# V Wo of all heads ahead of the first queries, the last FFN halves one step sooner, the last gates on ScalarE, the last deferred store behind the last transpositions

## The chip, the cores and the metric

The kernel runs on one core of a Trainium2 chip. The time is the device time of one execution in microseconds; the median of three runs of the kernel before is 559.36 (559.25, 559.36 and 560.31). The profile is of one further execution. In what follows PE is TensorE, DVE is VectorE, ACT is ScalarE, POOL is GpSimd and SP is SyncE.

## What is computed

```python
xn  = layernorm(x)                                  # 2048 x 448
q   = xn @ wq                                       # 16 heads of 256
k,v = the last 512 rows of the caches               # 8 heads, each used by two query heads
s   = concat_h(softmax(q k^T / 16) v) @ wo          # 2048 x 448
g   = silu((gelu(xn @ w_gate) * (xn @ w_up)) @ w_down)
out = x + s * g
```

## The kernel before

The kernel has no scheduler: a small planner (`Plan`) records operations in the order in which the Python code names them, gives each engine its own in that order, and derives the semaphore waits from declared buffers. What an engine does first is therefore decided by the order of the code alone. All matmuls go through one line, L384 in `mms`, so they are told apart by their operands (bank<-kT,qT are scores, bank<-xq,wq and wqr queries, bank<-vw,pT and vw,sS the product with V Wo, bank<-wd,actT the FFN's down product, bank<-woa,vTa or wob,vTb V Wo itself). ScalarE's plain activations go through L378, plain DMAs through L372, transposing DMAs through L375.

The work has three stages.

First, the FFN: layernorm, gate and up products, gelu, and the down product of each of 16 row tiles of 128. A down product is two halves of seven matmuls 128x448 (`down_mm`), and behind the second half ACT's tanh (L378) and a DVE operation (L581) make the gate of that tile (`down_gate`), which `store_g` sends to DRAM.

Second, for each of 16 heads, V Wo is computed ahead, so that the attention product is with V Wo instead of V and Wo in turn. `vw_head` runs four pairs of matmuls into four PSUM banks; each is evacuated by ACT (L713, L719) and, for two of the four, by DVE as well (L715); DVE's three sums (L726) follow. L713 of the second pair waits until L715 of the first has read what it shares. The heads are put between the down halves of tiles 8 to 13 in the list `order`. Head 13 uses banks 2, 3, 6 and 7, heads 14 and 15 both use banks 0 to 3. Between heads 14 and 15 stand the queries of steps 0 and 1 (banks 7 and 6) and ACT's evacuation of them to qT (`q_evac`).

Third, the attention loop: 128 steps, one for each block of 256 rows and each head. Step n computes the scores S(n) of two tiles of 128 rows (`s_jobs`, PSUM banks 4, 5 and 6 in turn, so a tile takes the bank of the tile three before), the queries of step n + 2 (`q_jobs`; in the first four steps in banks 7 and 1, later in 7), and, from step 4 on, the product PV(n - 4) with V Wo (banks 0 to 3). The matmuls use 64 rows each; `halves` writes the order of the lower and the upper half of the rows, side by side. DVE then takes the row minimum of each tile (L852, the scores are negated), ACT the exponential (L857, with its sum), DVE the reciprocal (L863) and POOL the norm (L873). SP transposes the result, 256 rows at once, by DMA (L375) into pT, and three steps after its own step DVE makes four sums of it (L888, `sums`). PV multiplies pT and these sums by V Wo in seven products, as a fast matrix multiplication does, and sums over heads in PSUM.

In steps 0 to 3 there is no PV yet; behind their scores stand the four down halves of tiles 14 and 15 (banks 0 and 2), with the gates made in steps 1 and 3.

Once a block of 256 rows has had its 16 heads, its banks are evacuated (L947) and finished over the next nine steps: POOL sums (L955), DVE the gate (L964, into `tmp`), POOL the addition of x (L974, into `ofin`). Stores of the result and loads for the next tiles wait in a list `moves`, from which one is issued on SP's queue in each step.

The last block is handled apart. In step 125 POOL scales the last two gates into `tmp` (`gates_scaled`, L1034). After the loop the last step's norm is split (tile 0 by POOL, L1122, tile 1 by ACT), each with its own half transposition. The heads of the last four steps are multiplied directly, four matmuls 128x448 for each step and tile: eight for step 124, eight for step 125, then steps 126 and 127 for tile 14 and for tile 15. DVE and POOL (L1107) put the rest together, and SP stores tiles 14 and 15.

Of the kernel before, what the change touches and what calls it, by code (L numbers as in the profile page):

```python
# [5 lines left out]
ACT = mybir.ActivationFunctionType  # L6
ALU = mybir.AluOpType
# [159 lines left out]
def bass_recurrent_scan__sliding_block_cached__geglu_ffn__prompt_kernel(  # L167
# [36 lines left out]
    with es:  # L204
# [364 lines left out]
        def down_mm(t, o, wr, f0, f1):  # L569
            c, t4 = divmod(t, 4)  # L570
            mms([(o, actT[c % 2][:, f, t4 * P:(t4 + 1) * P], wd[:, f, :], f == 0, f == NF - 1)
                 for f in range(f0, f1)], [b_wd] + b_actT[c % 2], wr)
# [156 lines left out]
        def vw_head(h, banks, last=True):  # L729
            K.reuse(b_vw[h])  # L730
            for j, i in zip((0, 2, 1, 3), banks):
                vw_mm(h, j, i)
            if last:
                vw_sums(h)
# [61 lines left out]
        def halves(lo, up):  # L796


            t, todo = [0, 0], (list(lo), list(up))
            while todo[0] or todo[1]:  # L800
                u = 0 if todo[0] and (not todo[1] or t[0] <= t[1]) else 1
                i, c0, c1, l, r, st, sp, reads = todo[u].pop(0)
                t[u] += c1 - c0 + 6
                other = half_of[i][1 - u]
                half_of[i][u] = mms([(bank[i][:, c0:c1], l, r, st, sp)], reads, [b_ps[i]],
                                    [] if other is None else [other])
# [3 lines left out]
        def q_jobs(n, e):  # L810

            c, h = divmod(n, Hq)
            y, i = c % 2, bq(n)
            if e == 1 and 2 <= n < 2 + LAG:
                i = 1
            out = ([], [])
            reads = b_wql[h // HG] + [b_xq[y]]
            for u in range(2):
                rows = slice(R * u, R * u + R)
                for k in [2, 1, 0] + ([NK] if u == e else []):  # L820
                    l = wqr[rows, h, :] if k == NK else wq[rows, k, h * Dh + e * P:h * Dh + (e + 1) * P]
                    out[u].append([i, e * CW, (e + 1) * CW, l, xq[rows, y, k, :], False, False, reads])
            return out
# [100 lines left out]
        def flat(x):  # L924
            return [z for y in x for z in y]
# [69 lines left out]
        for k in order:  # L995
            if isinstance(k, float):
                t, f = int(k), 0 if k == int(k) else NF // 2
                i = 4 + t % 2
                down_mm(t, bank[i][:, 0:D], [b_ps[i]], f, f + NF // 2)
                if f:  # L1000
                    down_gate(t, bank[i][:, 0:D], [b_ps[i]])
                    store_g()
            elif k < 14:
                vw_head(k, banks4())
                if k in (8, 10):
                    y = k // 10
                    K.reuse(b_xq[y:y + 1])
                    load_xq(y)
            elif k == 14:
                vw_head(k, (0, 1, 2, 3))  # L1010
                js = [[q_jobs(n, e) for e in range(2)] for n in range(2)]
                js[0][0][1][0][5] = js[1][1][0][0][5] = True
                js[0][0][0][-1][6] = js[1][1][1][-1][6] = True
                halves(js[1][1][0] + js[1][0][0], js[0][0][1] + js[0][1][1])
                halves(js[0][1][0] + js[0][0][0], js[1][0][1] + js[1][1][1])
                K.reuse(flat(b_qT))
                for n in range(2):
                    q_evac(n)
            else:
                vw_head(k, (0, 1, 2, 3))  # L1020
        K.reuse(b_p32 + flat(b_pn) + b_pT[:3] + flat(b_sS[:2]) + b_tmpr + b_g2r)

        VW12 = {NST - Hq + 6 + i: Hq - LAG + i for i in range(LAG)}
# [5 lines left out]

        ends_at = ((NT - 2) % NXR, (NT - 1) % NXR)  # L1030

        def gates_scaled():
            for s, y in enumerate(ends_at):
                K.op("pool", lambda e, s=s, y=y: e.tensor_scalar(  # L1034
                    tmp[:, s, :], gr[:, y, :], sc[:, 1:2], 1.0, op0=ALU.mult, op1=ALU.mult),
                    (b_gr[y], b_sc), (b_tmp[s],))

        todo, stores, ready, last_sum = [], [], [], []
        for n in range(NST):
            h, m = n % Hq, n - LAG  # L1040
            c = n // Hq
            more = n + 2 < NST
            ends = m >= 0 and m % Hq == Hq - 1
            if n == LAG:
                store_g()
                K.reuse(b_pT[3:] + b_sS[2])
            s0, s1 = s_jobs(n, 0, True), s_jobs(n, 1, not more)
            for t in ready:
                store_out(t)
            ready, stores = stores, []  # L1050
            if moves:
                moves.pop(0)()
            if more:
                q0, q1 = q_jobs(n + 2, 0), q_jobs(n + 2, 1)
                q0[1][0][5] = True
                (q1[0] if m >= 0 else q1[1])[-1][6] = True
                if m < 0:
                    q1[0][0][5] = q0[0][-1][6] = True
            if m < 0:
                halves(s0[0] + q1[0] + q0[0] + s1[0], q0[1] + s1[1] + s0[1] + q1[1])  # L1060
                t, i, f = NT - 2 + n // 2, n // 2 * 2, n % 2 * NF // 2
                down_mm(t, bank[i][:, 0:D], [b_ps[i]], f, f + NF // 2)
            else:
                one, two, all_ = pv_plan(m)
                if more:
                    halves(s0[0] + one + q0[0] + q1[0] + s1[0] + two, q0[1] + q1[1] + s0[1] + s1[1] + all_)
                else:
                    halves(s0[0] + s1[0] + all_, one + s0[1] + s1[1] + two)
            if n >= 1:
                recip(n - 1)  # L1070
                norm(n - 1)
            row_min(n, 0)
            if more:
                q_evac(n + 2)
            if ends:
                evac(0, "dve")
                evac(2, "act")
            row_min(n, 1)
            expo(n, 0)
            expo(n, 1)  # L1080
            if 3 <= n < NST - 1:
                last_sum = [sums(n - 3, (0, 1, 2, 3))]
            if n in (1, 3):
                i = n // 2
                down_gate(NT - 2 + i, bank[2 * i][:, 0:D], [b_ps[2 * i]])
            if n == 2:
                store_g()
            if n in VW12:
                vw_plain(VW12[n])
            if n == NST - 3:  # L1090
                gates_scaled()
            if n == LAG:
                K.reuse(b_aS + b_tmp + b_ofin + b_xr + b_gr)
                for t in range(NXR):
                    load_fin(t)
            if ends:
                evac(1, "dve")
                evac(3, "act")
                todo.extend(finish(m // Hq, "pool"))
            elif todo:  # L1100
                todo.pop(0)[1]()
            if h == 2 and c >= 1 and c + 1 < NC:
                load_xq(c + 1)
        assert not todo and not stores and not ready and not moves

        def add(eng, o, a, b, reads, writes, f=ALU.add):
            K.op(eng, lambda e: e.tensor_tensor(o, a, b, f), reads, writes)  # L1107
# [23 lines left out]
        norm_tile(0, "pool")  # L1131
        K.op("dve", lambda e: e.tensor_copy(aS[:, 0:2, :], two(bank[0][:, 0:D])), (b_ps[0],), b_aS[0:2])
        norm_tile(1, "act")
        act(a[5], bank[2][:, HN:D], ACT.Copy, (b_ps[2],), b_aS[5:6])
        add("pool", a[1], a[0], a[1], b_aS[0:2], b_aS[1:2])
        add("dve", a[2], bank[1][:, 0:HN], a[0], [b_ps[1], b_aS[0]], b_aS[2:3])
# [1 line left out]
        add("dve", a[6], a[6], a[5], b_aS[5:7], b_aS[6:7])  # L1138
        add("dve", a[3], bank[1][:, HN:D], a[2], [b_ps[1], b_aS[2]], b_aS[3:4])
        add("dve", aS[:, 4:6, :], two(bank[2][:, 0:D]), aS[:, 3:4, :].broadcast_to([P, 2, HN]), [b_ps[2], b_aS[3]], b_aS[4:6])  # L1140
        gs = [two(tmp[:, s, :]) for s in range(2)]
        xs = [two(xr[:, q, :]) for q in ends_at]
        for i, k in ((1, 0), (6, 1)):
            add("pool", a[i], a[i], gs[0][:, k, :], [b_aS[i], b_tmp[0]], b_aS[i:i + 1], ALU.mult)
            add("pool", a[i], a[i], xs[0][:, k, :], [b_aS[i], b_xr[ends_at[0]]], b_aS[i:i + 1])
        o = aS[:, 4:6, :]
        add("dve", o, o, gs[1], b_aS[4:6] + b_tmp[1:2], b_aS[4:6], ALU.mult)
        add("dve", o, o, xs[1], b_aS[4:6] + [b_xr[ends_at[1]]], b_aS[4:6])
        PB = (7, 5)
        for n, t in [(n, t) for n in range(NST - LAG, NST - 2) for t in range(2)] + [  # L1150
# [8 lines left out]
        for t in range(2):  # L1159
            i, sl = PB[t], (slice(1, 7, 5), slice(4, 6))[t]  # L1160
            p = two(p32[:, t, 0:D])
            add("dve", p, two(bank[i][:, 0:D]), gs[t], [b_ps[i], b_tmp[t]], (b_p32[t],), ALU.mult)
            add(("pool", "dve")[t], two(ofin[:, t, :]), p, aS[:, sl, :], [b_p32[t]] + [b_aS[k] for k in ((1, 6), (4, 5))[t]],
                (b_ofin[t],))
            store_out(NT - 2 + t)
            moves.pop(0)()
# [55 lines left out]
```

## Time and profile before

| what | us |
|---|---|
| median of three runs | 559.36 |
| the profiled execution | 560.09 |
| its span, first to last instruction | 558.30 |
| granted TensorE clock | 1.000 |
| PE busy | 548.5 (98%) |
| DVE, ACT, POOL busy | 462.3, 341.3, 261.5 |
| first score matmul | starts at 158.67 |
| last matmul issued from | 549.74 to 554.47 |

Times in the profile are microseconds from the span's start. The page gives each engine's busy time, the chain of work that ended last, followed back from the end, and the costliest groups of instructions; the views of the trace give stretches of time, single instructions and who waited for whom. A matmul's row is its start and a modelled end, and matmuls overlap: two on different row halves run side by side, and the next starts before the last has ended. So what PE loses is read from the distance between starts, not from its busy share. DMA rows of SP are the issue alone; when the data has landed is told apart.

### The profile page before, as it was taken

To read this page: it belongs to the slowest core of one execution; us is meant where nothing else is said; L and a number is where in the kernel's file an instruction comes from. 1 tells how busy PE (TensorE), PEld (TensorE's weight loads), DVE (VectorE), ACT (ScalarE), POOL (GpSimd) and SP (SyncE) were. 2 spreads that over 40 slices of the span, in tenths; PEclk is the share of its full clock that TensorE was granted. 3 is DMA by queue.
4 is the path that set the end of the run, shared out by engine and by line. 5 is a ranking of instruction groups with operands and counts; after the bars stand their busy time and mean duration, and the time that the engine had idled before them with its cause. 6 is when DMAs were issued, how large, how long until landed. Compare 5 with 4: busy or idle time off the path is not lost.

```text
span 558.3 us, 18692 instructions
## 1 busy us (share of the span) xinstructions
PE 548.5 (98%) x7612; PEld 425.5 (76%) x7612; DVE 462.3 (83%) x1177; ACT 341.3 (61%) x811; POOL 261.5 (47%) x376
## 2 busy tenths in 40 slices
PE   8999999999999999999999999999999999999996
PEld 5544444445557999998899899999999998998883
DVE  6674979767767778898898889899888988988996
ACT  5432324467776766766767667676676666676662
POOL 1121590100004443765565476557537646654675
PEclk9999999999999999999999999999999999999999
DMA  9998999601106776478647756845865666584465
GB/s 268 182 239 148 226 310 145 128 1 44 37 18 109 121 114 108 83 105 126 100 87 138 123 78 114 127 98 94 140 104 88 111 127 106 90 139 95 79 101 85
DMA packets 187653, 66.07 MB, mean 118 GB/s; under 512 B 169120, under 2 KB 184624, under 8 KB 187568
## 3 DMA queue, kind: packets, MB, share of 16 engines
q1 hardware_dynamic: 184336, 56.96, 60.1%
q0 software_dynamic: 2464, 7.34, 4.5%
q8 instruction: 60, 0.98, 0.8%
q10 hardware_dynamic: 768, 0.57, 0.3%
q14 instruction: 25, 0.20, 0.2%
HBM read 19.76 MB, written 5.77 MB: 46 GB/s over the span
## 4 chain that ended last, share of the span: by engine, by line
PE 88%; DVE 7%; ACT 2%; issue 2%; DMA 1%; POOL 0%; DVEq 0%; ACTq 0%
PE bank L384 88%; DVE vw L726 1%; DVE vw L715 1%; DVE actT L559 1%; DMA pT<-pn 1%; ACT vw L713 1%; DVE mx L676 1%; DMA x<-in_A_x_dram 1%; DVE stats L431 1%; DVE xn L457 1%; ACT gl L378 0%; DVE sS L888 0%; DVE mn L852 0%; DVE g2a L581 0%; POOL rstd L443 0%
## 5 line engine op out<-in xcount | busy, mean ns | idle before, releaser
L384 PE MATMUL bank<-kT,qT 64*128 64x512 bf16 x1024 | 282.1, 376 | 0.5 <-ACT p L857 0.5
L873 POOL TENSOR_SCALAR pn<-p,rd 128x512 f16<-128x512 f32 x254 | 178.3, 714 | 177.8 <-DVE rd L863 177.8
L384 PE MATMUL bank<-xq,wq 64*128 64x256 bf16 x1536 | 220.9, 269 | 0.3 <-ACT vw L719 0.2
L384 PE MATMUL bank<-vw,sS 64*128 64x224 f16 x1984 | 217.5, 257 | 0.4 <-DVE sS L888 0.3
L384 PE MATMUL bank<-vw,pT 64*128 64x224 f16 (+1 forms) x1520 | 211.3, 259 | 2.0 <-DMA pT<-pn 1.5
L852 DVE TENSOR_REDUCE mn<-bank 128x1 f32<-128x512 f32 x256 | 173.3, 684 | 39.3 <-PE bank L384 33.5
L857 ACT ACTIVATE p<-bank,mn 128x512 f32<-128x512 f32 x256 | 174.8, 684 | 8.2 <-DVE mn L852 4.3
L384 PEld LDWEIGHTS bank<-vw,sS 64*128 64x128 f16 x1984 | 146.9, 94 | 19.2 <-PE bank L384 2.7
L384 PEld LDWEIGHTS bank<-xq,wq 64*128 64x128 bf16 x1536 | 141.5, 94 | 9.7 <-ACT vw L719 0.5
L384 PEld LDWEIGHTS bank<-vw,pT 64*128 64x128 f16 (+1 forms) x1520 | 142.2, 94 | 7.5 <-DMA pT<-pn 1.9
L378 ACT ACTIVATE qT<-bank 128x512 bf16<-128x512 f32 (+1 forms) x132 | 77.0, 584 | 115.9 <-PE bank L384 114.9
L384 PEld LDWEIGHTS bank<-kT,qT 64*128 64x128 bf16 x1024 | 86.9, 94 | 7.0 <-ACT p L857 1.2
L384 PE MATMUL bank<-xnT,wgu 64*128 64x512 bf16 (+2 forms) x768 | 84.4, 350 | 0.7 <-issue 0.4
L888 DVE TENSOR_TENSOR sS<-pT 128x256 f16<-128x256 f16 x248 | 73.4, 336 | 0.3 <-DMA pT<-pn 0.3
L384 PE MATMUL bank<-xq,wqr 64*128 64x256 bf16 x256 | 68.3, 269 | 0.0
L384 PEld LDWEIGHTS bank<-xnT,wgu 64*128 64x128 bf16 x768 | 36.7, 94 | 38.4 <-issue 1.2
L378 ACT ACTIVATE gl<-bank 128x512 bf16<-128x512 f32 x56 | 33.1, 597 | 48.6 <-PE bank L384 41.9
L857 ACT ACTIVATION_READ_ACCUMULATOR p<-bank,mn 128x1 f32 x256 | 50.7, 198 | 0.0
L559 DVE TENSOR_TENSOR actT<-bank,gl 128x512 bf16<-128x512 f32 x56 | 37.4, 686 | 15.6 <-PE bank L384 14.9
L888 DVE TENSOR_TENSOR sS<-sS,pT 128x256 f16<-128x256 f16 x124 | 46.8, 377 | 0.0
L384 PE MATMUL bank<-wd,actT 128*128 128x448 bf16 x224 | 45.4, 353 | 0.6 <-DVE actT L559 0.5
L955 POOL TENSOR_TENSOR aS<-aS 128x224 f32<-128x224 f32 (+1 forms) x35 | 29.8, 850 | 27.7 <-DVE rd L863 25.8
(82 smaller groups left out, 413.0 us busy)
## 6 DMA issues: line engine op xcount, KB each, us to landing
wq<-in_A_wq_dram POOLq DMA_DIRECT2D x8, 384.0 KB, 8.6
woa<-in_A_wo_dram POOLq DMA_DIRECT2D x6, 448.0 KB, 5.3
pT<-pn SPq DMA_TRANSPOSE x129, 3.1
xn_t<-xnT SPq DMA_DIRECT2D x16, 128.0 KB, 3.9
xq<-xn_t SPq DMA_DIRECT2D x8, 256.0 KB, 3.0
xr<-in_A_x_dram SPq DMA_DIRECT2D x16, 112.0 KB, 2.7
gr<-gate_t SPq DMA_DIRECT2D x16, 112.0 KB, 2.7
out_dram<-ofin SPq DMA_DIRECT2D x16, 112.0 KB, 2.0
```

Of the source, the lines that this page charges most:

```text
L378: K.op("act", lambda e, o=o, i=i: e.activation(o, i, func, scale=scale), reads, writes)
L384: ins = e.matmul(o, lhsT=l, rhs=r, start=st, stop=sp)
L431: K.op("dve", lambda e: e.bn_stats(stats[:, t, :], x4[:, t, :]), (b_x4[t],), (b_stats[t],))
L457: K.op("dve", lambda e: e.tensor_scalar(xn[:, s, lo:hi], x4[:, t, src:src + hi - lo], mv[:, t, 0:1], rstd[:, t:t + 1], op0=ALU.subtract, o ...
L559: K.op("dve", lambda e: e.tensor_tensor(actT[c % 2][:, f, :], bank[b + 1], gl[:, s, :], ALU.mult), (b_ps[b + 1], b_gl[s]), (b_actT[c % 2][ ...
L676: K.op("dve", lambda e: e.tensor_reduce(mx[:, i:i + 1], o, AX.XY, ALU.max, apply_absolute_value=True), (b,), (b_mx,))
L713: K.op("act", lambda e: e.activation(v[:, 0, jj, :], o[:, 0:HN], ACT.Copy, scale=sc[:, 0:1]), (b, b_sc), (b_vw[h][0],))
L852: K.op("dve", lambda e: e.tensor_reduce(mn[:, m:m + 1], bank[i], AX.X, ALU.min), (b_ps[i],), (b_mn[m],))
L857: K.op("act", lambda e: e.activation(p32[:, z, :], bank[i], ACT.Exp, bias=mn[:, m:m + 1], scale=-1.0, accum_out=rsum[:, 2 * r + t:2 * r + ...
L873: K.op(engs[t], lambda e, o=o, i=i, s=s: e.tensor_scalar(o, i, s, 1.0, op0=ALU.mult, op1=ALU.mult), (b_p32[z], b_rd[r]), (b_pn[y][t],))
L888: o = K.op("dve", lambda e, i=i, a=a, b=b, f=f: e.tensor_tensor(s[i], a, b, f), r, (b_sS[y][i],))
L955: K.op(eng, lambda e: e.tensor_tensor(sl[0], sl[1], sl[2], ALU.add), [b_aS[i] for i in a + b], [b_aS[i] for i in o], after=last_sum)
```

## The change

The program has the same matmuls. These things move:

- V Wo of head 15 is computed straight behind head 14, ahead of the queries of steps 0 and 1.
- The four down halves of tiles 14 and 15 stand one step sooner: the first ahead of step 0, the others behind steps 0, 1 and 2. The gates of tiles 14 and 15 are made in steps 0 and 2 (before: 1 and 3), and both are stored in step 2.
- In steps 0 to 3 the two lists given to `halves` begin with queries, and both score tiles end at the end of the step.
- The last two gates are scaled by ACT, in steps 120 and 123, into a place of their own (`gsl`, where V Wo of head 1 lay), instead of by POOL in step 125 into `tmp`.
- In the last two steps no move is issued. The one left, the store of tile 12, is issued behind the last half transposition.

```diff
-            elif k == 14:
-                vw_head(k, (0, 1, 2, 3))
-                js = [[q_jobs(n, e) for e in range(2)] for n in range(2)]
...
-                for n in range(2):
-                    q_evac(n)
             else:
                 vw_head(k, (0, 1, 2, 3))
+        js = [[q_jobs(n, e) for e in range(2)] for n in range(2)]
...
+        for n in range(2):
+            q_evac(n)
+
+        def fill(k):
+            t, i, f = NT - 2 + k // 2, (0, 2)[k // 2], k % 2 * NF // 2
+            down_mm(t, bank[i][:, 0:D], [b_ps[i]], f, f + NF // 2)
+            if f:
+                down_gate(t, bank[i][:, 0:D], [b_ps[i]])
...
-        def gates_scaled():
-            for s, y in enumerate(ends_at):
-                K.op("pool", lambda e, s=s, y=y: e.tensor_scalar(
-                    tmp[:, s, :], gr[:, y, :], sc[:, 1:2], 1.0, op0=ALU.mult, op1=ALU.mult),
-                    (b_gr[y], b_sc), (b_tmp[s],))
+        gsl, a, _ = place("gsl", [P, 2, D], F32, at=rv)
+        b_gsl = sbuf_bufs(a, D * 4, 2)
+        GS = {NST - 8: 0, NST - 5: 1}
+
+        def gates_scaled(t):
+            y = ends_at[t]
+            K.reuse(b_gsl[t:t + 1])
+            act(gsl[:, t, :], gr[:, y, :], ACT.Copy, (b_gr[y], b_sc), (b_gsl[t],), scale=sc[:, 1:2])
...
+        fill(0)
         for n in range(NST):
...
-            if moves:
+            if moves and n < NST - 2:
                 moves.pop(0)()
...
             if m < 0:
-                halves(s0[0] + q1[0] + q0[0] + s1[0], q0[1] + s1[1] + s0[1] + q1[1])
-                t, i, f = NT - 2 + n // 2, n // 2 * 2, n % 2 * NF // 2
-                down_mm(t, bank[i][:, 0:D], [b_ps[i]], f, f + NF // 2)
+                halves(q1[0] + s0[0] + q0[0] + s1[0], q0[1] + s1[1] + q1[1] + s0[1])
...
-            if n in (1, 3):
-                i = n // 2
-                down_gate(NT - 2 + i, bank[2 * i][:, 0:D], [b_ps[2 * i]])
+            if n < 3:
+                fill(n + 1)
             if n == 2:
                 store_g()
             if n in VW12:
                 vw_plain(VW12[n])
-            if n == NST - 3:
-                gates_scaled()
+            if n in GS:
+                gates_scaled(GS[n])
...
         norm_tile(1, "act")
+        while moves:
+            moves.pop(0)()
```

In the end's operations `gsl` replaces `tmp`; nothing else changes there.

More of the change, by code (lines that the diff above doesn't have):

```diff
@@ L1008, in bass_recurrent_scan__sliding_block_cached__geglu_ffn__prompt_kernel @@
                     load_xq(y)
-            elif k == 14:
-                vw_head(k, (0, 1, 2, 3))
-                js = [[q_jobs(n, e) for e in range(2)] for n in range(2)]
[L1012 to L1016, printed above, removed]
-                for n in range(2):
-                    q_evac(n)
             else:
                 vw_head(k, (0, 1, 2, 3))
+        js = [[q_jobs(n, e) for e in range(2)] for n in range(2)]
+        js[0][0][1][0][5] = js[1][1][0][0][5] = True
+        js[0][0][0][-1][6] = js[1][1][1][-1][6] = True
+        halves(js[1][1][0] + js[1][0][0], js[0][0][1] + js[0][1][1])
+        halves(js[0][1][0] + js[0][0][0], js[1][0][1] + js[1][1][1])
+        K.reuse(flat(b_qT))
+        for n in range(2):
[5 more added lines that the diff above has]
+                down_gate(t, bank[i][:, 0:D], [b_ps[i]])
         K.reuse(b_p32 + flat(b_pn) + b_pT[:3] + flat(b_sS[:2]) + b_tmpr + b_g2r)
@@ L1103, in bass_recurrent_scan__sliding_block_cached__geglu_ffn__prompt_kernel @@
                 load_xq(c + 1)
-        assert not todo and not stores and not ready and not moves
+        assert not todo and not stores and not ready
         def add(eng, o, a, b, reads, writes, f=ALU.add):
@@ L1140, in bass_recurrent_scan__sliding_block_cached__geglu_ffn__prompt_kernel @@
         add("dve", aS[:, 4:6, :], two(bank[2][:, 0:D]), aS[:, 3:4, :].broadcast_to([P, 2, HN]), [b_ps[2], b_aS[3]], b_aS[4:6])
-        gs = [two(tmp[:, s, :]) for s in range(2)]
+        gs = [two(gsl[:, s, :]) for s in range(2)]
         xs = [two(xr[:, q, :]) for q in ends_at]
         for i, k in ((1, 0), (6, 1)):
-            add("pool", a[i], a[i], gs[0][:, k, :], [b_aS[i], b_tmp[0]], b_aS[i:i + 1], ALU.mult)
+            add("pool", a[i], a[i], gs[0][:, k, :], [b_aS[i], b_gsl[0]], b_aS[i:i + 1], ALU.mult)
             add("pool", a[i], a[i], xs[0][:, k, :], [b_aS[i], b_xr[ends_at[0]]], b_aS[i:i + 1])
         o = aS[:, 4:6, :]
-        add("dve", o, o, gs[1], b_aS[4:6] + b_tmp[1:2], b_aS[4:6], ALU.mult)
+        add("dve", o, o, gs[1], b_aS[4:6] + b_gsl[1:2], b_aS[4:6], ALU.mult)
         add("dve", o, o, xs[1], b_aS[4:6] + [b_xr[ends_at[1]]], b_aS[4:6])
@@ L1161, in bass_recurrent_scan__sliding_block_cached__geglu_ffn__prompt_kernel @@
             p = two(p32[:, t, 0:D])
-            add("dve", p, two(bank[i][:, 0:D]), gs[t], [b_ps[i], b_tmp[t]], (b_p32[t],), ALU.mult)
+            add("dve", p, two(bank[i][:, 0:D]), gs[t], [b_ps[i], b_gsl[t]], (b_p32[t],), ALU.mult)
             add(("pool", "dve")[t], two(ofin[:, t, :]), p, aS[:, sl, :], [b_p32[t]] + [b_aS[k] for k in ((1, 6), (4, 5))[t]],
```

## The prediction

> **What bounds the kernel now.** The page comes first: TensorE (PE) is busy for nearly the whole span. A time is therefore won or lost only where PE waits.
>
> ```profile
> PE 548.5 (98%) x7612; PEld 425.5 (76%) x7612; DVE 462.3 (83%) x1177; ACT 341.3 (61%) x811; POOL 261.5 (47%) x376
> ```
>
> Second, the chain that ended last, asked for 150 to 182 us, where V Wo, the first queries and steps 0 to 4 lie (start, us, what):
>
> ```profile
> 155.16 0.41 DVE vw L726
> ...
> 155.90 0.38 DVE vw L726
> 156.28 0.37 DVE vw L715
> ...
> 157.65 0.97 ACT qT L378 x2
> ...
> 161.78 0.61 DVE mn L852
> ...
> 162.41 0.79 ACT p L857 x2
> ...
> 163.33 10.10 PE bank L384 x74
> ...
> 173.45 0.63 DVE g2r L581
> ...
> 174.13 7.87 PE bank L384 x100
> ```
>
> Until 163 the chain runs on DVE and ACT, which evacuate V Wo; PE joins late. After that PE sets the pace, apart from one wait for the gate of tile 15 (g2r). How much PE loses is read from the table of stretches (the first number after the stretch is its length):
>
> ```profile
> 158.67:160.84 2.17, 2.02 (x23) 1.18 (x23) 1.28 (x4) 2.06 (x5) 0.00 (x0) 1.00 0.00 0
> ...
> 162.27:164.72 2.45, 1.99 (x23) 1.32 (x23) 1.20 (x4) 1.73 (x5) 0.55 (x1) 1.00 0.00 0
> ...
> 166.15:167.89 1.74, 1.74 (x24) 1.36 (x23) 0.79 (x3) 1.14 (x4) 0.00 (x0) 1.00 0.68 133
> ...
> 172.48:176.38 3.90, 3.40 (x52) 2.72 (x53) 2.27 (x6) 1.76 (x5) 1.36 (x2) 1.00 0.44 97
> 176.38:179.37 2.99, 2.99 (x54) 2.75 (x49) 2.44 (x8) 2.02 (x6) 1.36 (x2) 1.00 0.70 132
> ```
>
> Steps 0, 1 and 2 do equal work; step 2, at 1.74, is undisturbed. So step 0 loses 0.43 and step 1 0.71. Step 4 takes 3.90 where step 5 takes 2.99: 0.91 lost. Together 2.05 us.
>
> Third, the same chain for the end:
>
> ```profile
> 542.17 0.62 DVE sS L888
> ...
> 542.84 1.96 PE bank L384 x25
> 544.80 4.89 DMA pT<-pn
> ...
> 549.74 4.73 PE bank L384 x24
> ```
>
> The last matmuls stand from 548.26 to 549.74 (the waits give 1.48) for the transposition of step 125, which POOL's norm let start at 544.80 and which took 4.89 us.
>
> **Head: V Wo of head 15 ahead of the queries.** No matmul is added or removed. Head 15 goes to banks 0 to 3, which head 14 also uses, so its first matmul waits for DVE's L715 of head 14. That one starts at 156.20, behind the sums of head 13, and ends at 156.65. Before, PE did the queries (155.18 to 157.05, 1.87) meanwhile. Now PE stands from 154.92 (last issue of head 14 at 154.73 plus the 0.19 between issues) to 156.72. Head 15 then needs bank 2, which L715 frees at 157.71, and ends issuing at 158.53; the queries follow to 160.40. Before, both were done and step 0 began at 158.67: PE is 1.73 behind.
>
> What it buys, with the filler counted (each down half takes 1.43, 160.84 to 162.27, whatever its place): the first half lies at 160.40 to 161.83. Its bank 0 is free at 159.23 and it hides the evacuation of qT (two of 0.54, from 160.52). Step 0 then starts at 161.83 with bank 1 long free, and its 0.43 is gone. The sums of head 15 end at 161.45, ahead of the scores, so row minimum and exp follow at once. In the trace of before, bank 4 came free 1.64 after the first row minimum began (161.69 to 163.33). With scores ready at 163.75 this gives 165.42, and step 1 asks for that bank 0.32 into a start at 165.00: 0.10 lost, where 0.71 was.
>
> The new order puts the queries first and both score tiles last, so less lies between scores and the next step's bank. The gate of tile 14 (tanh 0.54, then DVE 0.62, from 165.86) now stands ahead of step 1's row minimum: bank 6 is free at 168.77, wanted at 168.59, 0.18 lost in step 2. Step 3 loses 0.10 by the same count. Step 4 would start at 173.46, now directly behind step 3, with no down half between. DVE still owes the gate of tile 15 (173.12 to 173.74), a reciprocal, two row minima (1.28) and the first sum for PV(0) (0.28), so PE's first sum operand comes at 175.3. It is wanted some 1.0 into the step: 0.75 lost. A query wait of 0.1 is added. So the wait for g2r goes and one for the sums takes its place. POOL's norm runs there too and can hold a sum for 0.2 more.
>
> Head: +1.73 - 2.05 + 0.10 + 0.18 + 0.10 + 0.85 = +0.9; with POOL's 0.2, +1.1; **I take +1.0**. Below, -0.3 if no new wait appears (1.73 - 2.05); above, +1.9 if step 4 also stands behind slower sums for as long again. I choose the middle because each of its terms has a row.
>
> The added gap of 1.8 is the one place where the clock could speak against the change: the trace keeps a granted clock of 1.00 through the 1.48 gap (stretch 548 to 550). [...]
>
> **Middle: the gates on ACT.** Two new ACT instructions of 128x448, SBUF to SBUF, at steps 120 and 123. That form is not in the trace: between tanh 128x448 from PSUM (0.54) and norm 128x512 from SBUF (0.72). I take 0.6. Behind each stands only the next qT evacuation, before which ACT sits idle 1.01 in these steps (527.57, 536.94). So 0; uncovered, at most 0.7 each. The place, head 1's V Wo, was last read at step 117, so nothing is waited for.
>
> **Tail.** POOL loses two instructions that stood ahead of the norm of step 125:
>
> ```profile
> 541.98 1.30 POOL L1034 TENSOR_SCALAR tmp<-gr,sc 128x448 f32<-128x448 bf16 x2
> 543.26 1.46 POOL L873 TENSOR_SCALAR pn<-p,rd 128x512 f16<-128x512 f32 x2
> ```
>
> The DVE sum at 542.17 took 0.61 and ended 0.14 after the first of them; without one beside it such a sum takes 0.29. PE's 542.84 moves to 542.58: 0.26. The next sums, no longer beside POOL, end some 0.5 earlier, so PE's wait until 545.12 goes too: the last scores, exps and norms are 0.45 earlier. POOL starts the norm of step 125 at 542.6, and its transposition starts at 544.08 instead of 544.80.
>
> What it then takes decides. One by one, the 127 full transpositions of the loop land 3.05 after issue (median of 82) where no packet of the queue "instruction" starts 0.4 to 2.9 after the issue. They take 3.2 to 4.9 in all 32 cases where one starts 0.4 to 2.45 after. This one had a packet at +2.37. These packets come every 256 PE instructions or so (214 to 290 between the last thirty), so this one moves with PE: 0.39 earlier (0.45, less 0.06 because two waits of PE fall away ahead of it), while the transposition moves 0.72. With its lag unchanged it would stand at +2.70, among the 13 cases between +2.45 and +2.9, of which 7 took 3.05 and 4 over 4.6. But its lag was about the longest (288 instructions since the one before), and a usual one puts it up to a microsecond earlier: +1.7 to +2.7, mostly inside. Then it lands 4.0 to 4.9 after 544.08, near 548.73, and PE goes on at 548.78 instead of 549.74: **-0.95**. Clear of the packet it lands at 547.1. Then step 126's transposition (issued 546.5, landing 549.6) is late next, and the end is 1.65 earlier.
>
> [...]
>
> The store of tile 12 (issue 0.57, landing about 2) moves from 543.36 to behind the last transposition (about 550.4). It lands by 552.6, when the last POOL sum wants its buffer (about 552.6 too). The transpositions behind it were not late for it: that of step 124 landed after 3.05 beside it. I count 0; at most 0.3 for tile 14, which ends ahead of tile 15.
>
> **Sum.** +1.0 + 0 - 0.95 = +0.05 on the profiled 560.09 (span 558.30), 560.1. That run lies 0.73 above the median 559.36. Carried over, this gives 559.4. But part of the 0.73 may be the caught transposition: uncaught, the profiled end would be 1.25 earlier (PE then waits only for step 126's, to 550.1), and the tail's gain only 0.4, giving 559.36 + 1.0 - 0.4 = 560.0. I predict between the two, **559.6: no change**.
>
> **Rivals.** (1) *The tail comes clear*: +1.0 - 1.65, 558.7. For it: a packet at +2.46 to +2.53 left most transpositions alone. Against: the transposition gains a lead of 0.33 at most, and most packets that near caught theirs. (2) *The head costs little*: DVE and ACT take step 3's work faster than I count, so that step 4 does not wait; +0.15 - 0.95, 558.5. For it: with a down half between, before's sums came in time. Against: the order on DVE. (3) *Slower, by the packet alone*: the timed runs of before are not caught, those of the changed kernel are. PE then ends 0.3 later than in an uncaught before (553.5 against 553.2), and the head's 1.0 comes on top: 560.7. It decides from a packet 0.4 to 2.45 after the transposition of step 125. For it: two of the three times are near 559.3, the third and the profiled one near 560.2. Against: a difference of 0.9 is not the full 1.25. That the change doesn't do what it says speaks only through the first filler: had it had to wait for bank 0, qT would stay uncovered. Bank 0 is 1.2 us early.
>
> **Numbers.** Below and above 0.2% (1.12 us, about what a measurement of this kernel can tell from no change) lie 558.24 and 560.48. Forecast 0.45, of it 0.02 slower; (1) 0.20, of it 0.05 faster; (2) 0.15, of it 0.08 faster; (3) 0.20, slower. Faster 0.13, same 0.65, slower 0.22. The range holds (1) and (2) nearly whole and (3): 558.3 to 560.8.
>
> **What would show it.** PE standing from 154.9 to 156.7, no wait in step 0, a small one in step 1, a wait of 0.7 to 1.0 for the sums in step 4 and none for g2r; step 5 beginning near 177.3. At the end POOL's norm of step 125 straight behind that of step 124, its transposition issued about 3.4 ahead of where PE needs it, and its landing 3.05 or over 4 after issue. Wrong would be a step 4 without a wait, or a qT evacuation late behind a gate on ACT.

## The result, and the profile after

The changed kernel takes 560.48 us (median of 20 runs, 559.69 to 562.07), the kernel before 559.49 (median of 20 runs beside them). The ratio is 1.0018, with a 95% interval of 1.0010 to 1.0027: a loss of 0.18%. The prediction called anything within 0.2% no change, that is up to 560.48, so the result lies on the edge of it. The profiled run of the changed kernel took 560.30 (span 558.5), that of before 560.09 (span 558.30). So the two profiles differ by 0.2 us and the timed runs by 1.0. The first question is where the profile's 0.2 comes from; the second, why it is not the 1.0.

TensorE is again busy for nearly the whole span (first part of the changed kernel's page):

```profile
PE 548.0 (98%) x7612; PEld 424.6 (76%) x7612; DVE 463.1 (83%) x1177; ACT 342.3 (61%) x813; POOL 260.8 (47%) x374
```

To follow the difference through the run, compare when the first exp of each step starts (after minus before, us). A number that stays the same from one row to the next says that nothing was lost or won between them.

| step | after - before | what happened since the row above |
|---|---|---|
| 4 to 24 | +1.05 to +1.03 | the head |
| 32 | +1.30 | one wait of PE, 0.33, at 259.5 |
| 120 | +1.21 | slow drift back |
| 124 | +1.23 | the gates on ACT |
| 126 | +1.11 | the tail |
| 127 | +0.85 | the tail |
| PE's last wait ends | +0.20 | 549.94 against 549.74 |

V Wo itself ran 0.09 earlier than before, so the head cost 1.14, counted from there.

**The head.** The chain of the changed kernel, asked for 153 to 178 us (start, us, what):

```profile
156.19 0.38 DVE vw L715
...
156.61 0.57 PE bank L384 x2
...
159.54 13.46 PE bank L384 x124
...
173.03 0.62 DVE g2r L581
...
173.72 1.19 DVE mn L852 x2
174.91 0.42 DVE sS L888
```

Before, the chain ran on DVE and ACT up to 163 and PE worked beside it. Now PE enters the chain at 156.61: it stood until DVE's second pass over head 14 had freed a bank. Then PE sets the pace from 159.54 to 173.00 without a gap, where before it had lost 0.43 and 0.71 in steps 0 and 1. At 173 the chain leaves PE once more: gate, reciprocal, two row minima and a sum follow each other on DVE, and PE goes on at 175.37. The table of stretches shows the same (the first number after the stretch is its length): the stand ahead of head 15, steps 0, 1 and 2, and step 4 up to the first scores of step 5.

```profile
154.92:156.61 1.69, 0.05 (x1) 0.00 (x1) 1.56 (x5) 0.93 (x4) 0.00 (x0) 1.00 0.00 0
161.84:163.58 1.74, 1.74 (x24) 0.99 (x23) 0.00 (x0) 0.33 (x2) 0.00 (x0) 1.00 0.00 0
165.01:166.79 1.78, 1.78 (x24) 1.15 (x23) 0.33 (x1) 1.73 (x7) 0.00 (x0) 1.00 0.00 0
168.22:170.16 1.94, 1.94 (x24) 1.15 (x23) 0.29 (x2) 1.50 (x6) 1.01 (x2) 1.00 0.08 18
...
173.33:177.43 4.10, 3.55 (x54) 2.64 (x52) 3.81 (x11) 2.66 (x8) 2.58 (x4) 1.00 0.48 116
```

Steps 0 and 1 are undisturbed or nearly so (1.74 is the undisturbed length; step 3 takes that too), step 2 loses 0.20, step 4 takes 4.10 where 2.99 would do. In the first row PE did one matmul in 1.69 us, and the granted clock stayed at 1.00 through it and behind it. In a second profile of this kernel it didn't (below, "A second profile").

**The middle.** One transposition out of 127 took 5.52 us and was waited for (chain, 250 to 262 us):

```profile
253.90 5.52 DMA pT<-pn
...
259.55 2.53 PE bank L384 x33
```

A packet of the queue "instruction" (16 KB each; the last thirty of this trace come 226 to 289 matmuls and weight loads apart) starts 2.54 after its issue. Below, a transposition is called caught if it lands late beside such a packet, and clear if it doesn't. In before the transposition in the same place (252.83) had its packet at the same 2.54 and took 5.28; runs of that order in which it lands sooner (4.68 in the tail alone, below) pass this place 0.2 earlier. So both kernels lose here, the changed one some 0.2 more.

The gates on ACT cost 0.02 at most: 657 ns each, with nothing idle ahead of them (a group of the changed kernel, by line).

```profile
L378 ACT ACTIVATE gsl<-gr,sc 128x448 f32<-128x448 bf16 x2 | 1.3, 657 | 0.0
```

**The tail** (chain, 541 to 559 us):

```profile
543.43 1.87 PE bank L384 x23
545.31 4.59 DMA pT<-pn
...
549.94 4.73 PE bank L384 x24
```

Take the 1.23 of step 124 off, and the transposition of step 125 is issued at 544.08, 0.72 earlier than before. It is still caught: it lands after 4.59 instead of 4.89, with the packet 2.07 after the issue. PE stands for 0.82 ahead of PV(125), where it stood for 1.48. The tail won 1.03 us. Profile against profile this makes +1.14 for the head, -0.09 for the start, about +0.2 for the middle, -1.03 for the tail: +0.2.

### The profile page after: what moved, and what is told of

The parts are those of the page before. It is cut to its first block, busy times and chain, and to the rows that moved or that the text cites. A ratio compares the mean times of both kernels' runs of the same rounds, so it can differ in the third digit from the quotient of the medians.

```text
span 558.5 us, 18691 instructions
## 1 busy us (share of the span) xinstructions
PE 548.0 (98%) x7612; PEld 424.6 (76%) x7612; DVE 463.1 (83%) x1177; ACT 342.3 (61%) x813; POOL 260.8 (47%) x374
## 4 chain that ended last, share of the span: by engine, by line
PE 86%; DVE 7%; DMA 3%; issue 1%; ACT 1%; POOL 0%; SPq 0%; DVEq 0%; ACTq 0%
PE bank L384 86%; DMA pT<-pn 2%; DVE vw L715 1%; DVE vw L726 1%; DVE actT L559 1%; DMA x<-in_A_x_dram 1%; DVE mn L852 1%; ACT vw L713 1%; DVE sS L888 1%; DVE mx L676 1%; ACT gl L378 0%; DVE xn L457 0%; DVE stats L431 0%; DVE g2a L581 0%; POOL rstd L443 0%
## 5 line engine op out<-in xcount | busy, mean ns | idle before, releaser
L384 PE MATMUL bank<-kT,qT 64*128 64x512 bf16 x1024 | 279.2, 376 | 0.0
L384 PE MATMUL bank<-xq,wq 64*128 64x256 bf16 x1536 | 218.3, 269 | 0.1
L384 PEld LDWEIGHTS bank<-xq,wq 64*128 64x128 bf16 x1536 | 139.9, 94 | 11.3 <-issue 1.9
```

What stands on the lines that cost most here:

```text
L384: ins = e.matmul(o, lhsT=l, rhs=r, start=st, stop=sp)
```

## The experiments

Theory A: the head costs its 1.05 to 1.14 in every run; the tail's gain depends on whether the transposition of step 125 is caught by an instruction packet, and in the timed runs of before it is caught less than in the profiled one. Rivals: the tail's gain is real everywhere and the head costs more than its profile shows; or the packets only happen to stand beside slow transpositions and cost nothing. Each time is a median beside runs of the kernel before on the same chip (559.76 for the first four, 559.46 for the next four, 559.42 for the last four).

| kernel | us | ratio to before, 95% |
|---|---|---|
| head alone | 560.86 | 1.0022 (1.0013 to 1.0031) |
| tail alone | 559.60 | 0.9995 (0.9986 to 1.0003) |
| changed, tiny matmuls at the start | 562.51 | 1.0052 (1.0033 to 1.0072) |
| before, tiny matmuls at the start | 559.75 | 1.0006 (0.9993 to 1.0019) |
| changed, first sum early | 559.88 | 1.0011 (1.0002 to 1.0020) |
| changed, queries between heads 14 and 15 | 559.07 | 0.9995 (0.9986 to 1.0004) |
| the same, bank 7, first sum early | 558.30 | 0.9981 (0.9971 to 0.9990) |
| gates alone | 558.84 | 0.9993 (0.9984 to 1.0002) |
| before, tiny matmuls in PE's waits | 559.45 | 0.9996 (0.9986 to 1.0005) |
| changed, tiny matmuls in PE's stand | 559.39 | 1.0001 (0.9993 to 1.0010) |
| bank 7, last half late | 558.62 | 0.9986 (0.9977 to 0.9994) |
| changed, once more | 560.09 | 1.0016 (1.0007 to 1.0024) |

**The two halves of the change.** The head alone is the diff without the lines on `gsl`, `GS`, `moves` and `while moves`; the tail alone is those lines and no others.

> Head of the change alone (V Wo of heads 14 and 15 ahead of the queries, down halves one step sooner, queries ahead of the scores), gates and last store as before. In the changed kernel's profile step 4 begins 1.05 us later than before, which is what the added gaps of PE give (1.65 + 0.55 against 0.56 + 0.49). Theory A (the head costs this in every run, and the tail's 1.0 us of the profile is won back only against a run of before whose transposition of step 125 was caught): 559.4 + 1.05 = 560.5, level with the whole change. Rival (the tail's gain is real in the timed runs too, and the head costs twice what its profile shows): 561.4, slower than the whole change by 1.0.

> Tail of the change alone: gates of the last tiles on ACT in their own place, last store behind the last transpositions; head as before. Theory A: the timed runs of before do not wait for a caught transposition, so there is little to win: 559.0 to 559.5. Rival: the tail gives 1.0 in the timed runs as it did in the profile: 558.4. In the profile POOL's norm of step 125 stands straight behind that of step 124, and the transposition of step 125 is issued about 1 us further ahead of PE's need than in before.

The head alone costs 1.10 us in the timed runs, with an interval from 0.7 to 1.7, and 1.13 in its trace, counted from V Wo to step 5. The rival's 561.4 is out. The tail alone gives 0.16, with an interval from a gain of 0.8 to a loss of 0.2; its trace, from step 124 on, gives 1.15. So the head agrees with its profile, and the tail is less in the timed runs than between the two profiles. The end of the head alone isn't that of before, though: its transposition of step 125 lands after 4.54, with the packet at +1.91, and from step 124 on its trace is 0.34 ahead of before's. The 1.10 holds that as well.

**Gates alone.**

```diff
-            if n == NST - 3:
-                gates_scaled()
+            if n in GS:
+                gates_scaled(GS[n])
...
```

> The kernel before with only the gates of the last tiles on ACT; the store of tile 12 stays ahead of the last transpositions. Theory (the tail's gain comes from POOL, the store's place costs nothing): transposition of step 125 issued as in the tail alone, PE goes on within 0.1 of it relative to step 124, time within 0.2 of the tail alone. Rival (the store's 2 us of transfer hold the transpositions behind it): transposition of step 124 or 125 lands over 0.3 later than in the tail alone.

The transposition of step 124 lands 3.05 after issue with the store ahead of it (541.32 to 544.37) and that of step 125 4.58 (4.47 in the tail alone, caught by a packet in both). From step 124 on the trace gives 1.04, within 0.11 of the tail alone. The time lies 0.8 below that of the tail alone, but beside other runs, and the two intervals nearly coincide. The store's place cost nothing that shows.

**Moving the packets.** The packets come with the number of PE instructions (226 to 289 from one to the next, above), so instructions that do no work should move them against the transpositions. At first they went to the very start:

```diff
-        warm(9, 2, QC)
+        warm(5, 2, QC)
+        tiny(64, 2)
...
```

(`tiny(n, i)`, whose definition is left out here, runs n matmuls of 32 columns into bank i. In the kernel before it is `warm(4, 2, QC)` and `tiny(80, 2)`.)

> The changed kernel with four of PE's nine 512-column warm-up matmuls, at the very start, exchanged for 64 tiny ones: 60 matmuls and their weight loads more, about 120 PE instructions, so each packet of the queue 'instruction' should come some 4.3 us earlier against the work and miss the transpositions of steps 124 and 125. No work on data is changed. If packets catch transpositions and cost time: T(125) lands 3.05 after issue instead of 4.59, PE's wait of 0.82 ahead of PV(125) is gone, and the time falls from 560.4 to about 559.6 (the 0.27 of the wait at 259.5 may go or another may come). If the packet only happens to stand there: landing stays over 4, time 560.4.

> The kernel before with five of the nine warm-up matmuls exchanged for 80 tiny ones: 75 matmuls and weight loads more, about 150 PE instructions, packets some 5.4 us earlier, clear of the transpositions of steps 124 and 125. If the timed runs of before were caught like the profiled one: 1.25 less, 558.2. If they were not (theory A): unchanged 559.4, and its own profiled run 558.9 to 559.4 instead of 560.1, with PE's wait of 1.48 at 549.74 gone or cut to 0.4.

In both traces the transposition of step 125 now lands after 3.05 to 3.10 (before: 4.89 and 4.59), no packet starts in the 2.9 us behind its issue, and the wait at the end is for step 126's: 0.50 instead of 1.48 in the kernel before, 0.48 instead of 0.82 in the changed one. The resumption of PE at PV(126), after taking off the shift that each trace has at step 120, is 0.99 earlier in the one and 0.38 earlier in the other. So in both the packet did cost time. The totals don't serve, because PE lost time at the start as well. In the changed kernel (chain, 9 to 15 us) it stood for 2.06 us with nothing that the profile shows it waiting for, and the runs spread from 560.96 to 565.49. In the four above 563 the mean granted clock is 0.993 to 0.997, in the other four 0.998 to 1.000.

```profile
10.98 2.06 issue
13.03 2.04 PE bank L384 x35
```

Hence a second pair, with 40 tiny matmuls where PE stands anyway:

```diff
+                if k == 15:
+                    tiny(40, 4)
                 vw_head(k, (0, 1, 2, 3))
...
```

> The changed kernel with 40 tiny matmuls (result never read) in PE's stand of 1.65 ahead of V Wo head 15: packets some 2.9 us earlier, clear of T(125), at about T(124) + 1.1, where a late landing harms nothing. If timed runs are caught like the profile: T(125) lands 3.05 after issue, PE then waits only for T(126), which the shift at the very start put at 0.35 less in the end: 560.5 - 0.35 = 560.1. If not caught: 560.5.

> The kernel before with 40 tiny matmuls (32 columns, result never read) put where PE stands anyway: 20 ahead of the first down tile (0.54 at 65.3) and 20 ahead of step 1 (0.56 at 163.3). That is 80 PE instructions more, so the packets of the queue 'instruction' come some 2.9 us earlier against the work: the one at T(125) + 2.37 to about T(125) - 0.5. In its profile T(125) should land 3.05 after issue and PE's wait of 1.48 at the end fall to 0.5, the wait for T(126). If the timed runs of before are caught like its profile: 559.5 - 1.0 = 558.5 (up to 0.2 more for the tiny ones). If they are mostly not caught: 559.5, no change.

> The changed kernel once more, unaltered, beside the others on one chip. All theories: 560.5 within 0.4, 1.0 above before; T(125) caught again with PE's wait near 0.8 (its packet is set by the count of PE instructions). Whether the wait of 0.33 at 259.5 comes back tells if that one belongs to the change's order or to the run.

In the changed kernel the 40 go into the stand of 1.65, of which 0.54 is left; they cost nothing. Its chain at the end, 541 to 559 us:

```profile
548.14 0.70 POOL pn L876
...
548.91 3.26 DMA pT<-pn
...
552.22 3.21 PE bank L384 x16
```

The chain now goes through the transposition of step 126, which POOL's norm released, and only 16 matmuls are left behind it, not 24: that of step 125 came in time. The time is 559.39, beside 560.09 for the unaltered changed kernel on the same chip: 0.7 less, with nothing else changed. The intervals of the two ratios just overlap. Against the first profile of the changed kernel the trace accounts for 0.37 at the end, against the second, where the transposition of step 125 took 4.42, for 0.2. In the middle the transposition that was waited for at 259.5 now takes 3.78, and PE passes this place 0.24 earlier than in the second profile. So the traces show 0.4 of the 0.7. In the second profile the wait of 0.33 at 259.5 is one of 0.07 (at 260.9), though the transposition was again caught there (5.29): its size belongs to the run.

In the kernel before, the first 20 did not go where they were meant to: PE lost 0.6 between 35 and 53 us, ahead of the first down tile, where it had not been waiting. The second 20 were free. The transposition of step 125 is clear (3.09), PE waits 0.54 for that of step 126, and the time is 559.45, no change. With the 0.6 that the first 20 cost taken off, it would be 558.85.

**A second profile.** The profiled run of "changed, once more" took 561.43, 1.1 more than the first profile. From V Wo of head 14 to the first exp it loses 1.5, in one place (stretches of this run; the clock is the third number from the end, ahead of DMA's two):

```profile
155.04:156.68 1.64, 0.01 (x1) 0.00 (x1) 1.51 (x5) 0.88 (x4) 0.00 (x0) 1.00 0.00 0
...
158.24:161.65 3.41, 3.35 (x27) 1.63 (x26) 2.50 (x7) 1.23 (x3) 0.00 (x0) 0.50 0.00 0
```

The first row is PE's stand ahead of head 15, now 1.64. From 1.56 behind it the granted clock is 0.50 for 3.41 us, and the queries of steps 0 and 1 take 2.88 from first to last start, where they took 1.67. Three more profiles hold such a stand of 1.63 to 1.64 (head alone, first sum early, tiny matmuls at the start), and the clock stays at 1.00 there as in the first. In no other profile does the record of the clock show less than 1.00 ahead of the last matmul. So the changed kernel has a second cost that comes in some runs only. That the head's stand brings it is not shown: one trace has the low clock behind such a stand, four have the stand without it, and of the 21 timed runs of the head alone and of first sum early none has a mean granted clock under 0.998. By the mean granted clock this cost is rare: of the 32 timed runs of the changed kernel five have 0.995 to 0.997 (561.13 to 562.07), while none of the 97 runs of the kernel before beside the experiments is under 0.998. Without the two such runs the median of "changed, once more" is 560.05 instead of 560.09, so this is not what the moved packets won.

**The head's two waits.** First the wait of step 4:

```diff
+            if n == 3:
+                sums(0, (0,))
             row_min(n, 0)
...
-                last_sum = [sums(n - 3, (0, 1, 2, 3))]
+                last_sum = [sums(n - 3, (0, 1, 2, 3)[n == 3:])]
```

> The changed kernel with one DVE instruction moved: the first sum of step 0 (the one PE waits for in step 4) stands ahead of step 3's two row minima instead of behind them. Theory (step 4 stands for the sum because the gate of tile 15, a reciprocal and two row minima lie ahead of it on DVE): the sum comes at about 174.1 instead of 175.3, PE's 0.55 us at 175.4 is gone, step 5 begins 0.5 earlier and the time is 560.5 - 0.5 = 560.0. The row minima come 0.3 later; rival: exp(3) then frees its bank later and PE waits for scores instead, time unchanged at 560.5.

The rival came true. The chain of this kernel, 165 to 178 us:

```profile
173.85 0.19 DVE sS L888
174.04 1.20 DVE mn L852 x2
175.24 0.42 DVE sS L888 x2
175.66 2.35 PE bank L384 x30
```

The sum is there at 174.04, but the row minima start behind it, and PE now stands for 0.69 ahead of a scores matmul. The last link names a sum that ended at the same moment. What the matmul needs is its bank, which exp of step 3 frees at 175.50. Step 5 begins 0.04 earlier, relative to V Wo, than in the changed kernel. The median is 0.2 below that of the changed kernel run last, within the intervals. Two limits lay one behind the other.

Then the stand ahead of head 15:

```diff
             else:
                 vw_head(k, (0, 1, 2, 3))
+                if k == 14:
+                    js = [[q_jobs(n, e) for e in range(2)] for n in range(2)]
...
-            t, i, f = NT - 2 + k // 2, (0, 2)[k // 2], k % 2 * NF // 2
+            t, i, f = NT - 2 + k // 2, (7, 2)[k // 2], k % 2 * NF // 2
```

The first part alone is "queries between heads 14 and 15"; the second is added with the first sum early. With it the queries made in steps 0 and 1 go to bank 0 instead of 7 (not shown).

> The changed kernel with the first queries back between V Wo of heads 14 and 15; the down halves stay one step sooner. Theory (the stand of 1.65 us for head 14's DVE pass is what the order of V Wo costs, and the queries were its cover): PE does not stand at 155 to 157; instead the first down half waits for bank 0 of head 15 until about 159.5, 0.8 us. Step 0 then starts 0.9 earlier than in the changed kernel: 560.5 - 0.9 = 559.6. Rival (DVE bounds this stretch whatever PE does, so the wait only moves to the scores): 560.5.

> As q_between, and the down halves of tile 14 in bank 7, which is free from 158.6 (the queries of steps 0 and 1 take bank 0 instead), and the first sum of step 0 ahead of step 3's row minima. Theory: no stand for V Wo, none for bank 0, none for the sum: 560.5 - 1.7 - 0.5 = 558.3, faster than the kernel before by 1.2. Rival (DVE's sums of head 15, done at 161.8, hold the row minima, so the scores' banks come late): step 1 waits for its bank, 559.0 to 559.5.

With the queries back, PE stands 0.82 for bank 0 at 159.7, as expected, and the trace's head is 0.20 behind before instead of 1.14. The time is 559.07. With bank 7 for the down halves the 0.82 is gone as well, and the head is 0.83 ahead of before. The wait of 0.69 for the bank of the scores is there as with the first sum early. At 558.30 this version is faster than both kernels, by 0.2% of the kernel before (0.1% to 0.3%).

Last, the filler against that 0.69:

```diff
-            if n < 3:
-                fill(n + 1)
+            if n in (0, 1, 3):
+                fill((1, 2, None, 3)[n])
```

(tile 15 in bank 3, the first sum in its old place, so three things differ from the version before it)

> As q_bank7_sum (558.3), but the wait that moved there from the sum to the scores (0.69 at 173.7, a bank that exp of step 3 frees late) is attacked by the filler: the last down half stands between steps 3 and 4 again, tile 15 in bank 3, which PV needs last, with its gate on DVE behind the sums of step 0. Theory (step 4 stands because DVE owes the gate, two row minima and a sum there with no PE work to cover them): no wait in step 4, 558.3 - 0.7 = 557.6. Rival (the row minima, exps and banks of steps 2 and 3, now back to back, take over): wait in step 3 of 0.2 to 0.5, 558.0 to 558.3; or PV(0) waits for bank 3 as before waited for g2r.

No wait is left in step 4, but the rival has its own (chain, 165 to 178 us):

```profile
169.35 0.52 PE bank L384 x6
169.87 0.06 ACT p L859
169.93 0.52 issue
170.44 0.20 ACT p L859
...
170.78 7.25 PE bank L384 x78
```

Steps 2 and 3, now back to back, wait 0.31 for a query's evacuation and 0.73 for an exp. The head is 0.39 ahead of before, 0.44 less than with the halves one step sooner; the time, 558.62, agrees. Of the two places tried, the one of the change is the better for the last half.

## Why the prediction was right, and where it was not

**The head, +1.0: right, but for the clock.** Measured +1.14 in the trace, +1.10 for the head alone. The stand was put at 1.80 and took 1.65, ending at 156.61 instead of 156.72. The stalls of steps 0 and 1 went as said. Small waits of 0.10, 0.18 and 0.10 were expected in steps 1 to 3; 0.04, 0.20 and 0 came. Step 4 waited for the first sum, seen at 175.33 where 175.3 was forecast, and step 5 began at 177.43, not 177.3. Rival (2), a head that costs little, failed at that wait. The sum has no term for the clock; the trace of before showed a granted clock of 1.00 through a gap of 1.48, and no run showed it for one of 1.8. In the first profile it stayed at 1.00 through 1.65; in the second a stand of 1.64 is followed by 3.41 us at 0.50, and the kernel loses 1.5.

**The middle, 0: right for the gates** (657 ns instead of 600, no one late). That a caught transposition in the middle could cost 0.2 to 0.3 was not in the sum; in the profiles it took 0.2 from before and 0.5 from the changed kernel, against the kernels in which that transposition comes clear.

**The tail in the profile, -0.95: right.** The transposition was issued 0.72 earlier, as counted; its packet came at +2.07, inside 1.7 to 2.7; PE went on at 548.71 in before's time, forecast 548.78. The store cost nothing. Rival (1), the tail clear of the packet, did not come: the packet stands 1.87 to 2.08 behind the transposition in six of the seven other profiles that have the gates on ACT and no tiny matmuls, and 2.45 in the seventh; all seven are caught.

**The step that failed is the last: carrying the sum from the profile to the median.** The prediction gave 559.4 if the timed runs of before are caught like the profiled one, and 560.0 if not, and took 559.6 between them. Measured was 560.48, and 560.09 for the same kernel later, 1.0 and 0.7 above before. That this still counts as no change is in part luck: the loss is some four times the forecast 0.24, and at the very edge. Rival (3), a before that is not caught beside a changed kernel that is, came nearest with 560.7. The term that was mis-sized is the tail's 0.95: in the timed runs the tail alone gave 0.16 and the gates alone 0.62, both with intervals that hold no change. The prediction's own figure for a before that is not caught, a gain of 0.4, is nearer, and it was right to name the caught transposition as the reason. From the traces it follows again: 1.03 between two caught kernels, less the 0.97 that before wins when it is clear (mean of its two kernels with packets moved), plus the 0.37 that the changed kernel wins, is 0.43. With a head of 1.05 to 1.14 this leaves 0.6 to 0.7 between the two when both are clear; the kernels with packets moved into PE's waits stand 0.5 apart (559.39, and 558.85 after the correction). With before clear and the changed kernel caught, rival (3)'s case, the same numbers give 1.14 - 1.03 + 0.97 = 1.1. A clear before ends 0.97 earlier than the profiled one, where the prediction counted 1.25, and a clear changed kernel 1.03 + 0.37 = 1.40, where it counted 1.65.

What stays open: how often the timed runs of before are caught, so theory A is not shown. Its packet at +2.37 lies near the edge of the lags that catch (in its profile all 32 transpositions with a packet at 0.4 to 2.45 are late, and 7 of the 13 from there to 2.9 are not), and the kernel with the packet moved away is only 0.6 faster after the correction, half of the 1.2 that its trace wins at the end (0.97) and in the middle (0.21). The other kernels don't agree on it: the changed kernel's 1.0 is what a clear before would give, while the head alone, itself caught, would then be 1.13 + 0.97 - 0.34 = 1.8 slower than before, and it is 1.1 (0.7 to 1.7). That fits a mixture, and as well a before that is caught every time but less late than in its profile; only one run of before left a trace, and its times show no two groups 1 us apart. Part of the profiled run's 0.7 above the median may as well be the spread of the start: PE's wait near 29.6 us lasts from nothing to 1.33 in the profiles of these kernels.

## What to carry to other kernels

The order that took PE's cover away from an evacuation put a wait of 1.65 in its place: the queries between the last two heads were worth 0.9, and the early down halves paid only in a bank that was already free. When one wait is removed, look at what the next matmul needs and when; here two limits lay 0.1 us apart, and moving one instruction only changed the name of the wait. And a term that rests on one event of one profiled run (here a late transposition) should be carried to the median with its chance, not at its full size. The same holds for a term that one profile shows as nothing: the granted clock stayed at 1.00 behind the head's stand in the first profile of the changed kernel and was 0.50 for 3.41 us in the second.

## What the runs showed of the hardware

The transposition of step 125 was late because of the instruction packet that it met, not merely beside it. In the changed kernel's first profile the transpositions with no packet 0.4 to 2.9 us after issue landed after 3.05 (median of 80), those with one at 0.4 to 2.45 after 3.86 (median of 32, up to 4.89). Adding 80 PE instructions moved the packet off that of step 125, and it landed in 3.10 instead of 4.42 to 4.59. So the count of PE instructions far ahead of this transfer was worth 0.2 to 0.4 us at the end of the changed kernel's traces, and about 1.0 in the kernel before's.

Forty tiny matmuls cost nothing inside a wait of 1.65 us, of which 0.54 was left, but 64 of them in the first 6 us were followed by a stand of PE of 2.06 us that no engine explains; the two profiles with such a block there show 1.14 and 2.06. What held PE was not shown.

The granted clock stayed at 1.00 through and behind a stand of 1.63 to 1.65 us in four profiles. In a fifth, with a stand of 1.64, it fell to 0.50 from 158.24 to 161.65, and the kernel lost 1.5 us. No trace here tells what sets the one case apart from the four.
